# K's weights loaded once and copied to the other half of the partitions by SyncE

## The chip, the core and the metric

The kernel runs on one core of a Trainium2 chip. The core has a matrix engine (TensorE, PE in the profile, its weight loads PEld), three engines for the rest (VectorE: DVE, ScalarE: ACT, GpSimd: POOL), an engine that only issues and synchronizes (SyncE: SP), and 16 DMA engines that serve the transfers which any of them issues. The metric is the device time of one execution in microseconds (us), the median of several runs.

## What is computed

Input x is 8 sequences of 4160 tokens with 192 values in f32. First a causal convolution of 7 taps, with softmaxed weights of each of 8 heads; then a channel mix on its result y:

```python
x_prev = x shifted by one token
xk = mu_k * x + (1.0 - mu_k) * x_prev
xr = mu_r * x + (1.0 - mu_r) * x_prev
k = np.maximum(xk @ w_k, 0.0)          # 192 -> 1024
v = k * k @ w_v                        # 1024 -> 192
r = 1.0 / (1.0 + np.exp(-(xr @ w_r)))  # 192 -> 192
return r * v
```

Here x stands for the convolution's result. The weight of this case is `w_k`, 192 x 1024 in f32, called `wk` in the kernel.

## The kernel before

**Two sequences side by side.** The sequences are taken in four pairs. Of a pair, one sequence lies in partitions 0 to 63 and the other in 64 to 127; the 192 channels are three chunks of 64. A matmul of K uses 64 rows of the array, so two of them, one for each sequence, lie beside each other. That is why `wk` (L179, 128 partitions x 3 chunks x 1024 columns, bf16) holds the same numbers twice, in the lower and in the upper half.

**Steps, slots and bundles.** A pair is cut into steps of 512 tokens; the first step of the first pair has 256. K of a step is made in slots: a slot fills one PSUM buffer with 1024 columns. For the first step a slot covers a quarter of `wk` (256 columns) for 256 tokens, so that slots 0 to 3 need quarters 0 to 3 in turn; later slots cover 128 columns for 512 tokens. For each slot `k_mm` (L465) runs its matmuls, for each chunk first on the lower and then on the upper half; `k_relu` (L489) moves the result out through ScalarE, and `k_square` (L495) squares it on VectorE. Four slots are a bundle. Four PSUM buffers go round among K, the convolution, r and v.

**The order is written out by hand.** Each engine runs its instructions in the order of the program text. `prologue` (L694) issues the first loads, prepares the masks and warms TensorE; `bundle_first` (L738) runs the convolution of the first two groups of x and slots 0 to 3; `bundle_second` (L766) runs slots 4 to 7 and the convolution of group 2; `bundle_rest` goes on from there.

**Who loads what at the start.** The first rows of x come as f32 by ScalarE's and SyncE's queues (`load_x_first`), with the tap weights and `mu`. SyncE then has nothing to issue until the first output. GpSimd issues all loads that change f32 into bf16 under way, in this order: x of group 1 (L712), the quarters of `wk` (L716), x of groups 2 and 3, `wr`, `wv`, x of group 4. `load_wk` (L196) is called once for each quarter and issues two loads of it, one to each half of the partitions; each reads the same part of `w_k` in HBM:

```python
        for c0 in range(0, DF, DF // 4):
            load_wk(c0, c0 + DF // 4)
```

The program's text names no semaphore: the framework makes an instruction wait for the transfers and instructions that wrote what it reads.

Of the kernel before, what the change touches and what calls it, by code (L numbers as in the profile page):

```python
# [14 lines left out]
def kernel(  # L15
# [11 lines left out]
    nc = tc.nc  # L27
# [4 lines left out]
    DF = moe_w_k.shape[1]  # L32
    P = 128
    NF = DF // P
    Q = 64
    NC = D // Q
# [142 lines left out]
    wk = const.tile([P, NC, DF], BF16)  # L179
# [14 lines left out]
            )  # L194

    def load_wk(c0, c1):  # L196
        for st in range(2):
            nc.gpsimd.dma_start(
                out=wk[st * Q : (st + 1) * Q, :, c0:c1],
                in_=bass.AP(  # L200
                    tensor=moe_w_k.tensor,
                    offset=moe_w_k.offset + c0,
                    ap=[[DF, Q], [Q * DF, NC], [1, c1 - c0]],
                ),
            )

    def load_wr():
        load_thirds(wr, moe_w_r, D)
# [485 lines left out]
    def prologue():  # L694
# [21 lines left out]
        for c0 in range(0, DF, DF // 4):  # L716
            load_wk(c0, c0 + DF // 4)
# [183 lines left out]
```

## Time and profile before

| | before |
|---|---|
| time, median of 3 runs | 417.33 us (417.06 to 418.06) |
| span in the profile | 417.0 us |
| GpSimd's DMA queue (q0) | 38704 packets, 14.66 MB |
| SyncE's DMA queue (q1) | 95138 packets, 48.32 MB |
| HBM read and written | 29.89 MB, 36.99 MB |
| loads of `wk` | 8 of 96 KB as written, median 4.7 us from issue to landing |
| mean relu of a slot (L493) | 1038 ns |

The page gives for each engine its busy time, then the span in 40 slices with a digit for the busy tenths of each. Lines of the timeline read: start, duration, engine, source line, operation, output from inputs, shapes, number of instructions, and in brackets the idle time before, with what released the engine. "DMA to landing" is the time from the start of the issuing instruction until the data have arrived. A share of the DMA engines can exceed 100%, since packets overlap within an engine. The chain of waits that the page gives is the work that ended last, followed back from the end.

### The profile page before, as it was taken

Reading aid. Unit: us, or ns where it says so; the run is one execution under the profiler, and the core shown is the slowest. Engines: PE = TensorE matmul, PEld = TensorE weight load, DVE = VectorE, ACT = ScalarE, POOL = GpSimd, SP = SyncE. Lnnn points to the kernel's source line nnn. Section 1 sums busy time; section 2 is a strip of 40 time slices with the busy share of each in tenths; the row PEclk is TensorE's granted clock in tenths of the full one; section 3 lists DMA queues with packets and bytes.
Section 4 is the critical chain, followed back from the end, with each engine's and each line's share of the span. In section 5 each row is a group of like instructions: output and inputs, shape, how many; then the busy total and the mean of one; then the engine's idle time right before and its main releaser. Section 6 shows DMA issues by size and latency. Waiting matters only on the chain.

```text
span 417.0 us, 16363 instructions
## 1 busy us (share of the span) xinstructions
PE 406.8 (98%) x7135; PEld 316.5 (76%) x7136; DVE 377.9 (91%) x672; ACT 347.8 (83%) x408; POOL 52.0 (12%) x79
## 2 busy tenths in 40 slices
PE   7889999999999999999999999999999999999996
PEld 5557777777887777778778877877777787777886
DVE  5888789999999999999999999999999999999984
ACT  6789898898898889889888888988898788877781
POOL 8750003102030100202002010201100000000000
PEclk9999999999999999999999999999999999999999
DMA  9999879958599694959879694797955564411223
GB/s 148 164 191 185 155 215 195 230 139 162 140 185 237 160 190 123 133 169 185 186 139 195 182 174 125 147 234 136 186 105 149 139 160 124 118 62 56 77 79 115
DMA packets 134715, 64.59 MB, mean 155 GB/s; under 512 B 84191, under 2 KB 134643, under 8 KB 134643
## 3 DMA queue, kind: packets, MB, share of 16 engines
q1 hardware_dynamic: 95138, 48.32, 45.4%
q0 software_dynamic: 38704, 14.66, 31.1%
q8 instruction: 56, 0.92, 0.9%
q10 hardware_dynamic: 800, 0.57, 0.5%
q14 instruction: 17, 0.13, 0.1%
HBM read 29.89 MB, written 36.99 MB: 160 GB/s over the span
## 4 chain that ended last, share of the span: by engine, by line
PE 91%; ACT 2%; issue 1%; DVE 0%; ACTq 0%
PE ps_v L566 40%; PE ps_k L481 38%; PE ps_r L538 7%; PE ps_c L299 5%; ACT k_sb L493 1%; PE ps_v L521 1%; ACT y L345 0%; DVE o_sb L582 0%; PE ps_t L390 0%; DVE o_sb L602 0%; ACTq L307 0%; ACTq L345 0%; ACTq L574 0%
## 5 line engine op out<-in xcount | busy, mean ns | idle before, releaser
L493 ACT ACTIVATE k_sb<-ps_k 128x1024 bf16<-128x1024 f32 x260 | 261.2, 1038 | 55.0 <-PE ps_k L481 54.9
L481 PE MATMUL ps_k<-xk,wk 64*128 64x512 bf16 (+1 forms) x1632 | 200.7, 367 | 1.9 <-DMA wk<-in_moe_w_k_dram 1.9
L507 DVE TENSOR_TENSOR k<-k_sb 128x1024 bf16<-128x1024 bf16 x260 | 177.7, 688 | 16.0 <-ACT k_sb L493 8.9
L566 PE MATMUL ps_v<-wv,k 64*128 64x192 bf16 x4032 | 188.8, 243 | 0.6 <-ACT k_sb L493 0.2
L566 PEld LDWEIGHTS <-k 64*128 64x128 bf16 x4032 | 172.4, 94 | 13.6 <-issue 1.2
L481 PEld LDWEIGHTS <-wk 64*128 64x128 bf16 x1632 | 87.9, 94 | 52.2 <-DMA wk<-in_moe_w_k_dram 2.6
L582 DVE TENSOR_TENSOR o_sb<-ps_v,r_sb 128x768 f32<-128x768 f32 x64 | 61.2, 957 | 11.1 <-PE ps_v L566 4.5
L126 POOL DMA_DIRECT2D xb<-in_x_dram x34 | 30.7, 907 | 192.4 <-PE ps_c L299 92.3
L546 ACT ACTIVATE r_sb<-ps_r 128x768 bf16<-128x768 f32 x65 | 54.6, 843 | 0.0
L345 ACT CAST y<-ps_c 120x960 bf16<-120x960 f32 (+4 forms) x67 | 50.7, 787 | 1.7 <-PE ps_c L299 1.7
L538 PEld LDWEIGHTS <-xr 64*128 64x128 bf16 x780 | 36.1, 94 | 12.3 <-issue 1.6
L538 PE MATMUL ps_r<-wr,xr 64*128 64x192 bf16 x780 | 44.0, 243 | 1.2 <-issue 1.1
L299 PE MATMUL ps_c<-xb,toe 64*128 64x480 bf16 (+2 forms) x240 | 39.2, 335 | 0.4
L455 DVE TENSOR_SCALAR xr<-d,mu 128x512 bf16<-128x512 bf16 (+1 forms) x102 | 35.6, 354 | 0.0
L455 DVE TENSOR_SCALAR xk<-d,mu 128x512 bf16<-128x512 bf16 (+1 forms) x99 | 33.2, 362 | 0.1
L424 DVE TENSOR_TENSOR d<-yT 128x1536 bf16<-128x1536 bf16 (+3 forms) x37 | 31.4, 849 | 1.4 <-ACT yT L329 1.4
L461 DVE TENSOR_TENSOR xr<-xr,yT 128x1536 bf16<-128x1536 bf16 (+1 forms) x33 | 31.0, 939 | 1.1
L461 DVE TENSOR_TENSOR xk<-xk,yT 128x1536 bf16<-128x1536 bf16 (+2 forms) x34 | 30.5, 898 | 0.1
L299 PEld LDWEIGHTS <-toe 64*128 64x128 bf16 x240 | 13.5, 94 | 12.4 <-issue 1.3
L408 POOL COPY y_tail<-yT 128x195 bf16<-128x195 bf16 x4 | 1.7, 430 | 68.7 <-DMA yT<-y_dram 68.7
L319 PEld LDWEIGHTS <-xb 128*32 128x32 bf16 (+3 forms) x264 | 4.9, 114 | 2.5 <-ACT xb L220 1.3
L108 POOL MEMSET xb<- 32x384 bf16 x3 | 1.3, 418 | 43.8 <-PE ps_k L481 43.8
(55 smaller groups left out, 62.8 us busy)
## 6 DMA issues: line engine op xcount, KB each, us to landing
out_dram<-o_sb SPq DMA_DIRECT2D x128, 192.0 KB, 2.7
y_dram<-y SPq DMA_DIRECT2D x10, 900.0 KB, 7.6
xb<-in_x_dram POOLq DMA_DIRECT2D x14, 480.0 KB, 8.3
xb<-in_x_dram POOLq DMA_DIRECT2D x6, 432.0 KB, 8.0
xb<-in_x_dram POOLq DMA_DIRECT2D x10, 192.0 KB, 5.6
y_dram<-y SPq DMA_DIRECT2D x3, 450.0 KB
y_dram<-y SPq DMA_DIRECT2D x1, 810.0 KB
wk<-in_moe_w_k_dram POOLq DMA_DIRECT2D x8, 96.0 KB, 4.7
```

What stands on the lines that cost most here:

```text
L299: nc.tensor.matmul(out=banks[:, bank, :, :, k * G : (k + 1) * G], lhsT=toe[q, h, :], rhs=xbs[g][q, :nb, :, h * G : (h + 1) * G], start=hal ...
L345: copy(out=bass.AP(tensor=y.tensor, offset=y.offset + d0, ap=[y.ap[0], [d1 - d0, 2], [2 * D, nb], [Q, 2], [1, n]],), in_=bass.AP(tensor=ps ...
L424: nc.vector.tensor_tensor(out=shaped(s, diffs[s][:, cs, :L]), in0=y_of(s, cs, 1), in1=y_of(s, cs, 0), op=ALU.subtract)
L455: nc.vector.tensor_scalar(out=t[:, c, :L], in0=diffs[s][:, c, :L], scalar1=mu[:, i, c : c + 1], scalar2=None, op0=ALU.mult)
L461: nc.vector.tensor_tensor(out=o, in0=o, in1=y_of(s, sl, 0), op=ALU.add)
L481: nc.tensor.matmul(out=ps[:, i, f * L : (f + 1) * L], lhsT=wk[r, c, fs], rhs=xk[r, c, :L], start=c == 0 and f == 0, stop=c == NC - 1 and f ...
L493: nc.scalar.activation(out=k_sb, in_=ps.rearrange("p a b -> p (a b)"), func=AF.Relu)
L507: nc.vector.tensor_tensor(out=o, in0=i, in1=i, op=ALU.mult)
L538: nc.tensor.matmul(out=ps[:, i, k * D : (k + 1) * D], lhsT=xr[q, c, ts], rhs=wr[q, c, :], start=c == 0, stop=c == NC - 1,)
L546: nc.scalar.activation(out=r_sbs[s, j], in_=ps[:, :, 0 : 2 * D], func=AF.Sigmoid)
L566: nc.tensor.matmul(out=v_ps[s, j][:, bank, k * D : (k + 1) * D], lhsT=k2s[s][q, f, t * P : (t + 1) * P], rhs=wv[q, f, :], start=half == 0 ...
L582: nc.vector.tensor_tensor(out=o_sb.rearrange("p (b t) d -> p b (t d)", b=2), in0=v_ps.pop((s, j)), in1=r_sbs.pop((s, j)), op=ALU.mult,)
```

## The change

`load_wk` loads each quarter only once, into partitions 0 to 63. A second transfer, issued by SyncE, copies the quarter from there to partitions 64 to 127, within on-chip memory and in bf16. It is for reading `w_k` from HBM and converting it once in place of twice, and for taking four transfers from GpSimd's queue. The copy of a quarter reads what the load wrote, so SyncE waits for that load before it issues it. The calls of `load_wk` and all else stay as they are.

```diff
     def load_wk(c0, c1):
-        for st in range(2):
-            nc.gpsimd.dma_start(
-                out=wk[st * Q : (st + 1) * Q, :, c0:c1],
-                in_=bass.AP(
-                    tensor=moe_w_k.tensor,
-                    offset=moe_w_k.offset + c0,
-                    ap=[[DF, Q], [Q * DF, NC], [1, c1 - c0]],
-                ),
-            )
+        nc.gpsimd.dma_start(
+            out=wk[0:Q, :, c0:c1],
+            in_=bass.AP(
+                tensor=moe_w_k.tensor,
+                offset=moe_w_k.offset + c0,
+                ap=[[DF, Q], [Q * DF, NC], [1, c1 - c0]],
+            ),
+        )
+        nc.sync.dma_start(out=wk[Q:P, :, c0:c1], in_=wk[0:Q, :, c0:c1])
```

## The prediction

> **What bounds the kernel now.** I read the page's busy table and slices first, then what touches K's weights (`wk`), then the timeline of TensorE and ScalarE at the start, and last what SyncE's plain transfers take when GpSimd's queue is full.
>
> The page (busy us with share of the span; then busy tenths in 40 slices of 10.4 us):
>
> ```profile
> PE 406.8 (98%) x7135; PEld 316.5 (76%) x7136; DVE 377.9 (91%) x672; ACT 347.8 (83%) x408; POOL 52.0 (12%) x79
> ...
> PE   7889999999999999999999999999999999999996
> ...
> DMA  9999879958599694959879694797955564411223
> ```
>
> TensorE is at 9 everywhere but in the first three slices and the last. The chain of waits is 91% TensorE. So a microsecond lost or won before about 25 us goes to the end nearly one for one, and elsewhere the change touches nothing. In the first four slices the DMA engines are full too.
>
> The view of the tile `wk`, first 60 us (who waited for it: us in total, times):
>
> ```profile
> L198 POOL DMA_DIRECT2D wk<-in_moe_w_k_dram x8: 628/628/687, 4.1 to 8.6; - x8
> ...
>   PEld L481: 2.6, 3
>   PE ps_k L481: 1.9, 2
>   POOL wv L211: 1.0, 1
> ...
> DMA to landing us min/median/max: 4.4/4.7/6.8
> ```
>
> GpSimd issues eight loads, 0.63 us each. TensorE loses 1.9 us in two waits. Where they lie, by TensorE's timeline (start us, us, instruction, [idle before, released by]):
>
> ```profile
> 10.49 1.59 PE L481 MATMUL ps_k<-xk,wk 64*128 64x256 bf16 x25
> 12.44 0.83 PE L481 MATMUL ps_k<-xk,wk 64*128 64x256 bf16 x11 [0.36 <-DMA wk<-in_moe_w_k_dram]
> 14.75 2.40 PE L481 MATMUL ps_k<-xk,wk 64*128 64x256 bf16 x24 [1.49 <-DMA wk<-in_moe_w_k_dram]
> 17.09 1.02 PE L319 MATMUL ps_t<-toe,xb 128*32 128x120 bf16 x64
> ```
>
> and ScalarE's beside it:
>
> ```profile
> 11.36 2.96 ACT L493 ACTIVATE k_sb<-ps_k 128x1024 bf16<-128x1024 f32 x3 [0.20 <-PE ps_k L481]
> 15.90 2.85 ACT L493 ACTIVATE k_sb<-ps_k 128x1024 bf16<-128x1024 f32 x3 [1.58 <-PE ps_k L481]
> ```
>
> The first four slots of K are of step 0 (256 tokens) and need one quarter of `wk` each. Taken one by one, the eight loads, issued at 4.14, 4.82, 5.44, 6.06, 6.68, 7.30, 7.92 and 8.56, took 4.6, 4.7, 4.5, 4.4, 4.4, 5.1, 6.8 and 6.4 us: they landed at 8.7, 9.5, 9.9, 10.5, 11.1, 12.4, 14.7 and 15.0. Slot 3 waits for the last two. The fourth relu starts at 15.90, and from there ScalarE is busy 4.85 of 5 us between 20 and 25 us: nothing downstream makes up lost time. **That start, 15.90, is the number to move.**
>
> **What a plain transfer takes here.** SyncE issues nothing between 2.8 and 30.2 us, so the trace has no such copy at the start. The nearest rows are output stores of 192 KB. Undisturbed, those at 58.86 and 59.30 landed in 2.0 and 2.7 us. Beside GpSimd's loads of x, the first, at 30.23, did this:
>
> ```profile
> L590 SPq DMA_DIRECT2D out_dram<-o_sb x1: 410/410/410, 30.2 to 30.2; - x1
> ...
> DMA to landing us min/median/max: 6.1/6.1/6.1
> ```
>
> The one at 30.68 took 7.3 us. Of two at 77.5 and 78.0 the trace tells one landing, 5.0; of two at 174.6 and 175.1 one, 5.2; two at 150.1 and 150.5 took 5.8 and 6.3. The DMA queues from 31.0 to 33.9 us show why (packets, MB, share of 16 engines; q0 is GpSimd's, q1 SyncE's):
>
> ```profile
> DMA packets 1466, 0.56 MB, mean 192 GB/s; under 512 B 1465, under 2 KB 1465, under 8 KB 1465
> ...
> q0 software_dynamic: 1465, 0.55, 159.5%
> ```
>
> Two stores had been issued, and not one packet of q1 moved in these 2.9 us. From 34.0 to 37.5 us q1 then moved 544 packets (0.39 MB) beside 750 of q0. So a transfer from SyncE first stands some 3 us behind what the engines have already taken from q0, and then shares about one for one.
>
> **What the Trainium skill says.** "DMA: Bandwidth & Descriptors", section "Queues, rings and completion order": each DMA engine goes round the queues that have work and leaves one only at a packet's end. The trace agrees with the sharing from 34 us on, and shows in addition the 3 us before it. The same page, "Two DMAs through the same engine are not ordered": a DMA that reads what another wrote must be issued after the completion semaphore of the first. So the copy adds its whole latency behind the load; no run here shows this pair yet. Same page, "SWDGE vs HWDGE vs iDMA": a cast during the transfer is GpSimd's alone; the loads here do go from f32 to bf16 on GpSimd, and the copy, bf16 to bf16, can go to SyncE. Same page, "Rules for kernel authors": transfers to the two partition halves use the same 16 engines, one transfer of 128 partitions is better. That fits the eight landings above, half a microsecond apart, but the change still makes two transfers of each quarter.
>
> **The change, part by part.**
>
> 1. *Four loads leave GpSimd.* 4 x 0.63 = 2.5 us of issuing. The loads of x for group 2 are issued at 6.7 in place of 9.2, and the wait of 1.0 us before `wv` goes, since fewer GpSimd transfers are in flight. Worth nothing by itself: x of group 2 landed at 16.0 and 17.0 (9.18 and 9.97 + 6.8 to 7.0) and its matmuls came at 17.09 behind K's; if K is late, x is early.
> 2. *The DMA engines' work.* Four loads less, at 0.58 us (8.74 to 10.46 is three of them) 2.3 us of q0. Four copies more: 64 partitions x 3 rows = 192 packets of 512 B each, 768 in all. Undisturbed, q1 moved 287 packets of 768 B in 0.7 us (60.2 to 60.9), so 1.9 us at most. An estimate from these rows: even to 1 us better. It hides behind the same x loads.
> 3. *The first halves.* They keep the places of the first four loads, so the quarters are in the lower partitions at 8.7, 9.5, 9.9 and 10.5. The lower half of quarter 3 comes 4.2 us earlier than now.
> 4. *The copies.* SyncE has finished its own issues at 2.8 and next issues at 30.2, so nothing is queued behind its four waits. Copy 0 goes out at about 8.8. Price: from 2.0 (undisturbed) to 7.3 (the worst above). At 8.8 GpSimd's queue holds three quarters and x of group 2, so I take the disturbed kind, and its lowest, 5.0, since a copy has half the bytes: **copy 0 lands at 13.8**. Copies 1 to 3 are issued by 11 and stand behind it. By bytes (0.39 MB in 3.5 us is 111 KB/us) 96 KB take 0.86 us, by packets (155 a us) 192 take 1.24; I take 1.05. **Copy 3 lands at 13.8 + 3 x 1.05 = 16.95**, against 15.0 for the last load now.
> 5. *The path.* Every slot needs the upper half with its second matmul. Slot 0 starts at 13.8 in place of 10.49. Now the fourth relu starts 0.94 us after the last load (15.90 - 14.96); so 16.95 + 0.94 = 17.9. The other way: slot 0 takes 0.85 us until its relu (10.49 to 11.36), then three relus of 1.03: 13.8 + 0.85 + 3.1 = 17.75. Both say the relu starts at 17.9 in place of 15.90: **+2.0 us**. VectorE's mixing of step 1 ends at 13.7 and isn't what is waited for.
>
> Sum: -0 (issuing) -0 (x earlier, hidden) +2.0 = 417.33 + 2.0 = **419.3 us**.
>
> **The rivals.**
>
> *The copies are hardly disturbed.* For: in a transfer between two parts of on-chip memory no HBM takes part, and a copy has half the bytes of the stores I price from. Against: 2.9 us without one packet can't be due to size. With 2.2 us, copy 0 lands at 11.0 and copy 3 at about 13.0. Then the relus set the pace: 11.0 + 0.85 + 3.1 = 14.95, or 1.0 us before now: 416.3, still within 0.3%. If the earlier x, `wr` and instruction fetches also remove TensorE's stop of 1.14 us at 22.97 (released by "issue", while 16 KB of instructions came through the crowded engines), it is 415.2. This is the case of a win.
>
> *About even.* A copy waits 1.5 us less than I take: 3.5 us, landings at 12.3 and 15.4. Then relu at 16.3, +0.4: 417.7.
>
> *Each copy stands in line on its own.* If every one of the four waits anew behind q0, say 2 us apart, copy 3 lands at 19.8, +4.8: 422. For: 7.3 us for the second of two stores. Against: those two ran without a pause once the first had started.
>
> **How the numbers follow.** Forecast (+1.3 to +3 us) 0.50; even (-1.2 to +1.2) 0.27, in which the undisturbed copy without the removed stop lies; a win of over 0.3% (1.25 us) 0.16; each on its own 0.07. The range from 416.2 to 421.4 leaves out most of the win's 0.16, where it goes below 416.2, and the worst, some 0.2 together. Faster 0.16, same 0.27, slower 0.57.
>
> **What would show it.** Four SyncE issues of `wk<-wk` at about 8.8 to 10.6, with 4.5 to 6.5 us to landing. TensorE's wait for `wk` at L481 up from 1.9 to about 5 us, the first at slot 0 (about 3.3 us), and its releaser the copy, not the load. GpSimd's loads of x of group 2 at 6.7. HBM read down from 29.89 by 0.79 MB, q1 up by some 770 packets. The fourth relu at about 17.9, and the distance to the end from there as now. I am wrong if the copies land within 3 us, if slot 0 starts before 12, or if the relu's delay is made up before 60 us.

## The result and the profile after

The changed kernel takes 421.64 us (median of 4 runs, 421.11 to 423.88), the kernel before 417.19 us beside it. The ratio is 1.0113, with a 95% interval from 1.0074 to 1.0152: **slower by 4.45 us, where 2.0 were forecast.**

The page of the changed kernel (busy us, share, instructions; busy tenths in 40 slices, with the granted TensorE clock in PEclk; then DMA queues with packets, MB, share):

```profile
PE 408.6 (97%) x7135; PEld 317.9 (76%) x7136; DVE 378.1 (90%) x672; ACT 347.6 (83%) x408; POOL 49.4 (12%) x75
...
PE   7699999999999999999999999999999999999996
...
PEclk9899999999999999999999999999999999999999
...
q1 hardware_dynamic: 95970, 48.72, 45.3%
q0 software_dynamic: 37872, 14.26, 30.2%
```

and the same line of the page of before:

```profile
PEclk9999999999999999999999999999999999999999
```

For TensorE the second slice (10.5 to 21.0 us) alone is worse than before. It also shows something that the page of before has nowhere: a granted TensorE clock below 9 tenths. HBM read is 29.10 MB, 0.79 less, as the halved loads must give.

The tile `wk` in the first 60 us, and TensorE's and ScalarE's timelines:

```profile
L205 SPq DMA_DIRECT2D wk<-wk x4: 590/608/735, 8.3 to 11.1; - x4
...
  PEld L481: 3.8, 2
  PE ps_k L481: 3.0, 1
```

```profile
10.79 0.28 PE L481 MATMUL ps_k<-xk,wk 64*128 64x256 bf16 x1
14.09 5.91 PE L481 MATMUL ps_k<-xk,wk 64*128 64x256 bf16 x59 [3.02 <-DMA wk<-wk]
19.93 1.02 PE L319 MATMUL ps_t<-toe,xb 128*32 128x120 bf16 x64
```

```profile
15.58 1.02 ACT L493 ACTIVATE k_sb<-ps_k 128x1024 bf16<-128x1024 f32 x1 [4.11 <-PE ps_k L481]
17.17 5.71 ACT L493 ACTIVATE k_sb<-ps_k 128x1024 bf16<-128x1024 f32 x6 [0.57 <-PE ps_k L481]
```

One matmul of slot 0, on the lower half, runs at 10.79; the next needs the copy and waits 3.02 us. Copies 0, 1 and 3 took 5.7, 6.4 and 6.5 us and landed at 14.04, 15.63 and 17.60 (the trace does not tell copy 2). The first relu above is slot 0's, at 15.58. Relus on end start 0.92 us apart, so the fourth starts at 17.17 + 2 x 0.92 = 19.01. What lay ahead of the copies is told by the DMA queues from 8.9 to 10.8 us, the first fence, and from 11 to 17 us, the second:

```profile
DMA packets 627, 0.24 MB, mean 127 GB/s; under 512 B 560, under 2 KB 627, under 8 KB 627
...
q0 software_dynamic: 627, 0.24, 116.2%
```

```profile
q0 software_dynamic: 2063, 0.77, 109.3%
q1 hardware_dynamic: 825, 0.39, 30.5%
```

Copy 0 was issued at 8.35, and until 10.8 no packet of SyncE's queue moved. Then nearly all of the four copies' packets (825 of 832, 0.39 MB) took six microseconds beside 0.77 MB of GpSimd's.

### The profile page after: what moved, and what is told of

It reads as the page before. It is cut to its first block, busy times and chain, and to the rows that moved or that the text cites. A ratio compares the mean times of both kernels' runs of the same rounds, so it can differ in the third digit from the quotient of the medians.

```text
span 419.2 us, 16367 instructions
## 1 busy us (share of the span) xinstructions
PE 408.6 (97%) x7135; PEld 317.9 (76%) x7136; DVE 378.1 (90%) x672; ACT 347.6 (83%) x408; POOL 49.4 (12%) x75
## 3 DMA queue, kind: packets, MB, share of 16 engines
HBM read 29.10 MB, written 36.99 MB: 158 GB/s over the span
## 4 chain that ended last, share of the span: by engine, by line
PE 90%; ACT 2%; issue 1%; DVE 0%; ACTq 0%
PE ps_v L566 40%; PE ps_k L481 38%; PE ps_r L538 7%; PE ps_c L299 5%; ACT k_sb L493 1%; PE ps_v L521 1%; ACT y L345 1%; DVE o_sb L582 0%; ACT r_sb L546 0%; DVE o_sb L602 0%; ACTq L307 0%; ACTq L345 0%; ACTq L574 0%; ACTq L493 0%
## 5 line engine op out<-in xcount | busy, mean ns | idle before, releaser
L481 PEld LDWEIGHTS <-wk 64*128 64x128 bf16 x1632 | 88.8, 95 | 54.3 <-DMA wk<-wk 3.8
L582 DVE TENSOR_TENSOR o_sb<-ps_v,r_sb 128x768 f32<-128x768 f32 x64 | 61.2, 956 | 11.2 <-PE ps_v L566 4.7
L319 PE MATMUL ps_t<-toe,xb 128*32 128x120 bf16 (+3 forms) x264 | 6.4, 272 | 0.4 <-ACT xb L220 0.4
```

The costliest lines, as they stand in the source:

```text
L481: nc.tensor.matmul(out=ps[:, i, f * L : (f + 1) * L], lhsT=wk[r, c, fs], rhs=xk[r, c, :L], start=c == 0 and f == 0, stop=c == NC - 1 and f ...
L582: nc.vector.tensor_tensor(out=o_sb.rearrange("p (b t) d -> p b (t d)", b=2), in0=v_ps.pop((s, j)), in1=r_sbs.pop((s, j)), op=ALU.mult,)
```

## The experiments

All times are against the kernel before in the same session (417.2 to 417.5 us). In the table "last quarter" is when the last part of `wk` was in place, and "to the end" is the span less the start of the fourth relu, all from the one profiled execution of each.

| run | last quarter | fourth relu | to the end | median us | ratio (95%) |
|---|---|---|---|---|---|
| e0 before again | 14.75 | 15.66 | 400.1 | 417.35 | 1.0001 (0.9991 to 1.0011) |
| the change | 17.60 | 19.01 | 400.2 | 421.64 | 1.0113 (1.0074 to 1.0152) |
| e1 after_warm | 18.32 | 19.43 | 400.2 | 421.54 | 1.0093 (1.0070 to 1.0116) |
| e2 after_drain | 13.76 | 17.14 | 402.7 | 421.88 | 1.0102 (1.0081 to 1.0123) |
| e3 after_gpcopy | 13.79 | 16.05 | 400.9 | 418.47 | 1.0018 (1.0008 to 1.0028) |
| e4 hold_short | 17.93 | 19.48 | 400.5 | 421.01 | 1.0084 (1.0052 to 1.0117) |
| e5 hold_short_warm | 16.46 | 17.37 | 400.3 | 419.64 | 1.0063 (1.0038 to 1.0088) |
| e6 half_dose | 19.55 | 21.09 | 400.6 | 423.90 | 1.0165 (1.0146 to 1.0185) |
| e7 two_copies | 19.63 | 23.37 | 400.3 | 425.27 | 1.0191 (1.0172 to 1.0210) |
| e8 unread | 15.43 | 16.34 | 402.1 | 419.00 | 1.0037 (1.0023 to 1.0051) |
| e9 no_copy | 10.12 | 13.86 | 400.2 | 415.97 | 0.9964 (0.9954 to 0.9973) |
| e10 pool_copy | 12.92 | 14.73 | 401.9 | 418.18 | 1.0014 (1.0002 to 1.0026) |
| e11 dve_copy | 14.78 | 15.70 | 400.6 | 418.09 | 1.0006 (0.9994 to 1.0019) |
| e12 two_dve | 11.63 | 13.74 | 401.2 | 416.82 | 0.9988 (0.9982 to 0.9995) |
| e13 reversed | 13.50 | 18.89 | 400.2 | 420.22 | 1.0064 (1.0048 to 1.0081) |
| e14 reversed_warm | 13.20 | 17.91 | 399.9 | 419.66 | 1.0056 (1.0040 to 1.0072) |

The parts of `wk` in the column "last quarter" are loads or copies, whichever came last. Where nothing later comes late, the column "to the end" is 400.2 within 0.4: a late fourth relu goes to the end one for one.

### A second profile of the kernel before (e0)

No edit.

> The kernel before, unchanged, for a second profile. In the first one TensorE stops for 1.14 us at 22.97 with no releaser but issue; the changed kernel has no such stop. If that stop belongs to the one execution that was profiled, it is absent here, the span is about 1 us shorter (416), and the profiles of before and after are then 3.3 us apart where the first two were 2.2, nearer to the 4.4 us of the times. If the stop belongs to the kernel before, it is here again at the same place, and the changed kernel gains about 1.1 us there. Time 417.2 either way.

The span is 415.8 against 417.0, and the stop at 22.97 shrinks to 0.28 us:

```profile
14.51 2.41 PE L481 MATMUL ps_k<-xk,wk 64*128 64x256 bf16 x24 [1.63 <-ACT k_sb L493]
...
23.01 0.50 PE L538 MATMUL ps_r<-wr,xr 64*128 64x192 bf16 x8 [0.28 <-issue]
```

```profile
15.66 2.86 ACT L493 ACTIVATE k_sb<-ps_k 128x1024 bf16<-128x1024 f32 x3 [1.20 <-PE ps_k L481]
```

So the long stop belonged to one execution. The fourth relu is at 15.66, which makes the change +3.35 there; the spans differ by 419.2 - 415.8 = 3.4, and so do the times of the two profiled runs (421.11 and 417.71).

### Only what stands ahead of the copies is changed (e2, e3, e4)

In e2 GpSimd reads the copied quarters before it goes on to x of group 2; in e4 it reads only the last loaded quarter; in e3 it issues the copies itself, ahead of x of group 2, and SyncE issues none.

```diff
 # e2
         make_toe()
+        hold = const.tile([P, DF // 4], BF16)
+        for c0 in range(0, DF, DF // 4):
+            nc.gpsimd.tensor_copy(out=hold[Q:P, 0:1], in_=wk[Q:P, 0, c0 : c0 + 1])
         load_x(2)
 # e4
+        hold = const.tile([P, 2], BF16)
+        nc.gpsimd.tensor_copy(out=hold[0:Q, 0:1], in_=wk[0:Q, 0, DF - 1 : DF])
         load_x(2)
 # e3
-        nc.sync.dma_start(out=wk[Q:P, :, c0:c1], in_=wk[0:Q, :, c0:c1])
...
             load_wk(c0, c0 + DF // 4)
+        for c0 in range(0, DF, DF // 4):
+            nc.gpsimd.dma_start(out=wk[Q:P, :, c0 : c0 + DF // 4], in_=wk[0:Q, :, c0 : c0 + DF // 4])
```

> The changed kernel, but GpSimd reads one column of each copied quarter (four copies of 64x1 into a spare tile) before it issues x of group 2, so that nothing but K's weights is in GpSimd's DMA queue while SyncE copies. Theory A (the copies stand behind x of groups 2 and 3 in the engines): copy 0 lands within 2.0 to 3.5 us of its issue in place of 5.7, copy 3 at about 13 to 14 in place of 17.6, TensorE's wait at slot 0 falls from 3.0 to under 1.5 us; then x of group 2, issued at about 13.5, comes at about 17 to 18 and sets the start of the convolution of group 2. Fourth relu at about 16, time 417 to 419. Theory B (a copy within on-chip memory takes 5 to 6 us whatever lies beside it): landings as in the changed kernel, copy 3 at 17, x of group 2 only then, time 424 or more.

> The four loads as in the changed kernel; the four copies are issued by GpSimd after them, ahead of x of group 2, in place of SyncE. Theory A (what costs is a second queue that gets its turn only after what the engines have taken from GpSimd's): in one queue the copies stand only behind the loads of K's weights, land 2.5 to 4 us after their issue, copy 0 at about 11.5, copy 3 at about 13.5 to 14.5; x of group 2 is issued at about 11.5 to 12 and lands at 16 to 18. Time 417 to 419. Theory B (the copy itself is dear): 5 to 6 us each, copy 3 at 17 or later, time 421 to 424.

> The changed kernel, but GpSimd reads one column of the last loaded quarter (lower half) before it issues x of group 2, so x of group 2 is issued at about 10.1 in place of 6.7 and most copies are in SyncE's queue first. Loads, copies and their issuer are as in the changed kernel. Theory A (the copies wait for what the engines have taken from GpSimd's queue, whoever issues them): copies land at about 12.4, 12.7, 13.5 and 14 to 15, fourth relu at 16.5 to 17.2 in place of 19.0, x of group 2 at about 16.5 to 17.5; time 418 to 419. Theory B (a transfer from SyncE behind one from GpSimd is dear in itself): copy 0 again after 5 us or more, time 421 or more.

The transfers `wk<-wk` of e2, first their times to landing, then the DMA queues from 9.95 to 13.5 us:

```profile
DMA to landing us min/median/max: 2.1/3.1/3.7
```

```profile
q1 hardware_dynamic: 832, 0.39, 44.3%
```

With only the loads of K's weights ahead of them, the same four transfers from SyncE land in 2.1 to 3.7 us, the last at 13.76. e3 has the same range from the other queue: 2.1 to 3.7 us, the last at 13.79. e4 shows both kinds within one run. Copies 0 and 1, issued at 9.5 and 10.3, ahead of x of group 2 (11.2), took 3.0 and 3.1 us; copy 3, issued at 12.5, behind it, took 5.4. So neither SyncE nor the on-chip copy is dear by itself: **what the copies wait for is the loads of x that were issued before them.**

The times were less well foreseen. e2's copies are early, but its slots run at a granted clock of 0.50 from 14 to 16 us, so that the fourth relu comes only 1.9 us earlier; and x of group 2, issued at 14.3, lands at 18.0 and 19.6, and TensorE stops 1.3 us for it. So it is 402.7 to the end, and the whole gain is gone. In e4 the last copy still stands behind x. e3 wins back 3.2 of the 4.2 us; what is left shows in the fourth relu, 0.4 us later than in e0, and in `wv`, which lands at 24.3 and keeps TensorE waiting for 0.8 us.

### Half the dose, and fewer, longer packets (e6, e7)

e6 loads quarters 0 and 1 twice, as before, and copies quarters 2 and 3 alone. e7 copies quarter 0, and then quarters 1 to 3 in one transfer.

```diff
 # e6
+        if c0 < DF // 2:
+            nc.gpsimd.dma_start(out=wk[Q:P, :, c0:c1], in_=...)
+        else:
             nc.sync.dma_start(out=wk[Q:P, :, c0:c1], in_=wk[0:Q, :, c0:c1])
 # e7
+        if c0 == 0:
             nc.sync.dma_start(out=wk[Q:P, :, c0:c1], in_=wk[0:Q, :, c0:c1])
+        elif c1 == DF:
+            nc.sync.dma_start(out=wk[Q:P, :, DF // 4 : DF], in_=wk[0:Q, :, DF // 4 : DF])
```

> Quarters 0 and 1 loaded twice by GpSimd as before, quarters 2 and 3 loaded once and copied by SyncE. Slots 0 and 1 start at about 10.7 as before, so TensorE does not idle ahead of slot 0. Theory A (the landing of the last copy sets the fourth relu): copies issued at about 11.3 and 12, 5 to 6 us each, copy 3 at 17 to 18, fourth relu at about 18 to 19, time 419.5 to 421. Theory B (what costs is the late slot 0 with four relus after it and the clock that is halved there): fourth relu at most 1 us later than before, time 418 to 418.5.

> The changed kernel with quarter 0 copied alone and quarters 1 to 3 in one copy of 64 partitions x 3 runs of 1536 bytes: half the packets, the same bytes. Theory A (SyncE's packets take turns with GpSimd's one for one, so it is the number of packets that counts): copy 0 at about 14, the second, issued at about 11, with 192 packets at about 15.5 to 16.3, against 17.6 for the last of four; then relus at ScalarE's pace from slot 0, or at the half clock's, fourth relu at 17.8 to 18.8, time 420 to 421. Theory B (bytes count, or the wait ahead of each transfer): the second lands at 17.5 or later, time 421.6 or more.

Half the copies cost more than all of them, and more than either expectation allowed. In e6 they are issued at 11.4 and 12.3, when x of groups 2 and 3 is in the queue whole (landing, then TensorE):

```profile
DMA to landing us min/median/max: 6.5/6.9/7.3
```

```profile
17.98 1.46 PE L491 MATMUL ps_k<-xk,wk 64*128 64x256 bf16 x12 [5.42 <-DMA wk<-wk]
```

Slots 0 and 1 were on time there, so a late slot 0 is not what costs: the last copy is. e7 lends no support to the idea of turns by packets: a third of the packets for the same bytes, and 8.3 us for the second transfer, about what copies 1 to 3 of the change took from the first issue to the last landing (9.2 to 17.6). It was issued 2 us later than copy 1 of the change, with more loads issued ahead of it, so whether bytes or packets count is not settled.

### The two halves of the change by themselves (e8, e9)

e8 is the kernel before with the four copies into a tile that nobody reads. e9 is the change without copies: K of the odd sequences takes its weights from the tile of the convolution's taps (`toe`), and so their output is not computed.

```diff
 # e8, on the kernel before
+        nc.sync.dma_start(out=wk2[Q:P, :, c0:c1], in_=wk[0:Q, :, c0:c1])
 # e9, on the change
-        nc.sync.dma_start(out=wk[Q:P, :, c0:c1], in_=wk[0:Q, :, c0:c1])
...
-                        lhsT=wk[r, c, fs],
+                        lhsT=wk[r, c, fs] if i == 0 else toe[r, (j * nf + f) % H, :],
```

> The kernel before, with its eight loads, and in addition SyncE's four copies of the lower half, into a tile that nothing reads. So the copies and their traffic are there, and no matmul waits for them. Theory A (the loss is the wait for the copies, not their traffic): copies land 5 to 8 us after their issue, TensorE does not wait for them, and the time is 417.2 to 417.9 (0.77 MB more traffic for a moment, up to 0.5 us on loads 7 and 8). Theory B (the copies slow the loads of x and of the instructions, and that is the loss): time 419 or more.

> The changed kernel without its copies: the four loads are halved as in the change, and K's second matmul of each pair (odd sequences) takes its weights from the tile of the convolution's taps in place of the upper half of wk; so the odd sequences of the output are not computed. It shows what the change would bring if the upper half came at no cost. Theory A (the removed loads had a price of their own, which the copies' wait outweighs): slot 3 is ready with the fourth load at 10 to 11, the fourth relu starts at 14.5 to 14.9 (ScalarE's pace), x of group 2 lands by 14, time 416 to 416.6. Theory B (the removal of the loads is worth nothing, since x of group 2 or ScalarE binds next): 416.9 to 417.5.

e9 takes 415.97 us: the four removed loads are worth 1.5 us (ratio 0.9964) where no copy has to be waited for. e8 takes 419.00: the copies' presence costs 1.5 us even where nobody waits for them. In its profile the last load of `wk` lands at 15.4 in place of 14.75, and that is 0.7 us of the path. The second half of x of group 2 lands at 18.4 in place of 16.7, but TensorE has no idle time for it. What more is lost there is TensorE's pace, which the next part is about: after a wait of 2.43 us the granted clock is 0.50 from 17 to 20 us, and 64 matmuls of the convolution take nearly twice as long, first in e0, then in e8:

```profile
16.85 1.02 PE L319 MATMUL ps_t<-toe,xb 128*32 128x120 bf16 x64
```

```profile
18.30 1.92 PE L321 MATMUL ps_t<-toe,xb 128*32 128x120 bf16 x64
```

The profiled execution (420.37) is one of five of e8's fifteen with a mean clock of 0.996 or less; the other ten have a median of 418.7, so without that loss the cost is some 1.2 us. The forecast had both parts at zero. They are not, and in these two kernels they are of equal size; e8's copies ran beside eight loads, though, so that they cancel in the change itself is not shown.

### TensorE's pace (e1, e5, e13, e14)

Each "warm" kernel runs matmuls of zeros ahead of slot 0, into the buffer that slot 0 starts anew: 14 in e1, 8 in e5 (which is otherwise e4), 18 in e14. e13 and e14 have no copies; they are the kernel before with the quarters loaded in reverse order, so that slot 0 waits for the last load.

```diff
 # e1, e5, e14 (n is the slot)
+        if n == 0:
+            for i in range(14):
+                nc.tensor.matmul(out=ps[:, i % 2, :], lhsT=ones_t, rhs=zeros, start=True, stop=True)
 # e13, e14
-        for c0 in range(0, DF, DF // 4):
+        for c0 in reversed(range(0, DF, DF // 4)):
```

> The changed kernel, with 14 matmuls of zeros ahead of slot 0 of K, so that TensorE works while it waits for the first copy. They write a PSUM buffer that slot 0 then starts anew, so the result is as before. Theory A (TensorE's idle 3.0 us halve its granted clock, which makes slots 0 to 2 take 1.3 us each in place of 0.65): the granted clock stays at 1.00 from 14 to 18 us, slot 1 is ready 0.6 us and the fourth relu about 0.8 us earlier (18.4 in place of 19.2), time 421.6 - 0.8 = 420.8. Theory B (only the copies' landings set the path, the clock is not on it): the clock may stay up, but the time stays at 421.6.

> As e4_hold_short, with 8 matmuls of zeros ahead of slot 0, so that TensorE has no idle stretch while it waits for copy 0. Theory C (the halved clock after an idle stretch is on the path when the copies land early, since slots then take 1.28 us each, more than ScalarE's 0.92): granted clock 1.00 throughout, fourth relu 0.7 to 1.1 us before that of e4_hold_short, time lower by as much. Theory D (the clock is not on the path): same time as e4_hold_short within 0.4 us.

> The kernel before with its eight loads in the reverse order of the quarters (3, 2, 1, 0). No copy and no other traffic; slot 0 now waits for the last load, at about 14.8, and TensorE idles some 4 us ahead of it. Theory C (idle before K halves TensorE's pace and that is on the path when all quarters are there): slots of 1.3 us each for some 3.4 us, fourth relu at about 19 to 19.5, 421 to 421.7. Theory D (pace is not on the path): relus at ScalarE's 0.92, fourth at 18.4, 420.2.

> As e13_reversed, with 18 matmuls of zeros ahead of slot 0 that fill TensorE's idle stretch. The loads are the same. Theory C: slots of 0.65 us, fourth relu at about 18.4, 0.7 to 1.1 us before that of e13_reversed, and the time lower by as much. Theory D: no difference of more than 0.4 us.

The matmuls of K in the changed kernel, in stretches of 2 us (us, TensorE busy and count, weight loads, granted clock, DMA share, GB/s):

```profile
14.00:16.00 2.00, 1.78 (x16) 0.98 (x18) 0.53 1.46 203
16.00:18.00 2.00, 2.00 (x26) 1.45 (x24) 0.61 1.52 197
```

After 3.0 us of idling the granted clock is about half, until 17.5. TensorE's timeline in e13, and then in e14:

```profile
13.27 6.98 PE L481 MATMUL ps_k<-xk,wk 64*128 64x256 bf16 x60 [2.02 <-DMA wk<-in_moe_w_k_dram]
```

```profile
10.29 4.06 PE L477 MATMUL ps_k<-zeros,ones_t 128*128 128x512 bf16 x18
14.28 4.09 PE L484 MATMUL ps_k<-xk,wk 64*128 64x256 bf16 x60
```

The same 60 matmuls take 6.98 us after an idle stretch of 2.0, and 4.09 without one. The zeros ran 1.1 us longer than the loads took to land (13.20), and still the fourth relu is 1.0 us earlier, 17.91 against 18.89. In the times that is 419.66 against 420.22, with overlapping ranges (419.29 to 420.90, 419.37 to 421.08): clear in the profiles, only suggested by the times. e5 is also below e4 (419.64, 421.01), but its last copy landed 1.5 us earlier as well, so most of that is not pace. "TensorE: Matmul & The Clock Gate" of the Trainium skill, section "What's actually happening", has the array at half rate once it has idled for a window of about 3.4 us. The half is seen here, but the length of the idling alone does not decide. In e13 2.0 us were enough; in e4 0.6 us, and K's first matmul there had taken 0.39 in place of 0.28 us already before that idling; in e0 slot 3 ran at full pace after 1.63 us. Slots 0 and 1 in e4, and then in e5:

```profile
12.53 2.74 PE L481 MATMUL ps_k<-xk,wk 64*128 64x256 bf16 x24 [0.60 <-DMA wk<-wk]
```

```profile
12.78 1.59 PE L484 MATMUL ps_k<-xk,wk 64*128 64x256 bf16 x25
```

The small matmuls of the convolution that ran before may be part of it (not tried).

On the path of the change it is worth little. From the last copy to the fourth relu it is 1.41 us in the changed kernel, 1.55 in e4 and 1.54 in e6, against 0.91 in e0 and e5, which ran at full pace: **0.5 us** by the profiles. The times do not show it: e1, where slots 0 and 1 ran at full pace, won nothing, and its last copy landed at 18.32 in place of 17.60.

### Copies without a transfer (e10, e11, e12)

e10 copies on GpSimd after x of group 2 is issued; e11 on VectorE, two quarters before the mixing of step 1 and two within it. e12 copies quarters 0 and 1 alone on VectorE and loads quarters 2 and 3 twice. SyncE copies nothing in the three.

```diff
 # e10
         load_x(2)
+        for c0 in range(0, DF, DF // 4):
+            nc.gpsimd.tensor_copy(out=wk[Q:P, :, c0 : c0 + DF // 4], in_=wk[0:Q, :, c0 : c0 + DF // 4])
 # e12, in bundle_first, ahead of slot 0 (e11 does the same by a helper)
+        for c0 in (0, DF // 4):
+            c1 = c0 + DF // 4
+            nc.vector.tensor_copy(out=wk[Q:P, :, c0:c1], in_=wk[0:Q, :, c0:c1])
 # e12, on the kernel before
-        for st in range(2):
+        for st in range(2 if c0 >= DF // 2 else 1):
```

> The four loads of the change; the upper half is copied by GpSimd itself (a tensor copy of 64 x 768 for each quarter, from partitions 0 to 63 to 64 to 127), after it has issued x of group 2. No second transfer, no place in any DMA queue. Theory A (a transfer's latency behind GpSimd's queue is the whole loss, so a copy without a transfer wins what the removed loads are worth): if such a copy takes 1.0 to 1.3 us, the quarters are there at about 9.7, 10.9, 12.1 and 13.3, the fourth relu starts at 14.3 to 14.8, x of group 3 is issued at 13.5 and still comes in time: 416 to 417. Theory B (the copies on GpSimd take 2 us or more each, or hold up its issuing of x of group 3, wr and wv): the fourth relu at 16 or later or a stop for wv, 417.5 to 420.

> The four loads of the change; the upper half is copied by VectorE, 64 x 768 for each quarter, quarters 0 and 1 after the mixing of step 0, quarters 2 and 3 between the parts of the mixing of step 1. No second transfer and nothing more on GpSimd. Theory A (the wait for a transfer is the loss; the removed loads are worth 1.5 us, as e9_no_copy showed): if a copy takes 0.3 to 0.5 us, the four relus of bundle 0 run on end from about 11.5, the mixing of step 1 ends at 14.7 to 15.5, and slot 4's relu, the first that feels it, starts at 15.5 to 16.3 against 16.6 in the kernel before; time 416.3 to 417.2, ahead of both kernels. Theory B (VectorE is full there and a copy takes 0.8 us or more): the mixing ends after 16.5, time 417.5 to 419.

> Quarters 0 and 1 loaded once and copied to the upper half by VectorE after the mixing of step 0; quarters 2 and 3 loaded twice by GpSimd as before: six loads, no transfer between halves. Theory A (two loads less take away most of what the last two loads cost, and VectorE has 0.5 us to spare ahead of step 1): copies of 0.5 us end at about 10.7, the sixth load lands at about 11.6 to 12.4, the four relus run on end, the fourth starts at about 14.3 to 14.6, the mixing of step 1 ends at 14.4 and slot 4's relu starts at 15.2 to 15.6 against 16.6 in the kernel before: 416.2 to 416.9, ahead of both kernels. Theory B (VectorE's 0.6 us comes back elsewhere, or the sixth load comes late on one engine): 417 to 418.

e10's quarters are there by 12.9 and its four relus run on end, but the next thing is late. VectorE's mixing of step 1 in e0, and then in e10 beside GpSimd's copies (9.5 to 12.9):

```profile
10.18 0.43 DVE L424 TENSOR_TENSOR d<-yT 128x512 bf16<-128x512 bf16 x1 [0.50 <-ACT yT L329]
10.64 0.43 DVE L455 TENSOR_SCALAR xk<-d,mu 128x512 bf16<-128x512 bf16 x1
11.11 0.45 DVE L461 TENSOR_TENSOR xk<-xk,yT 128x512 bf16<-128x512 bf16 x1
```

```profile
10.54 0.87 DVE L423 TENSOR_TENSOR d<-yT 128x512 bf16<-128x512 bf16 x1 [0.87 <-ACT yT L328]
11.44 0.80 DVE L454 TENSOR_SCALAR xk<-d,mu 128x512 bf16<-128x512 bf16 x1
12.28 0.92 DVE L460 TENSOR_TENSOR xk<-xk,yT 128x512 bf16<-128x512 bf16 x1
```

The same instructions take twice as long, and slot 4 waits for the mixing until 15.9. In e11 the last copy, queued behind VectorE's own work, ends at 14.8: no gain. e12 has two loads less and VectorE's half microsecond of idle time for the copies:

```profile
10.98 3.77 ACT L493 ACTIVATE k_sb<-ps_k 128x1024 bf16<-128x1024 f32 x4 [0.53 <-PE ps_k L481]
15.25 1.94 ACT L493 ACTIVATE k_sb<-ps_k 128x1024 bf16<-128x1024 f32 x2 [0.50 <-DVE k L507]
```

Four relus on end from 10.98, and 416.82 us against 417.50: **e12 is ahead of both kernels**; against the kernel before it is a ratio of 0.9988 (0.9982 to 0.9995), some 0.5 us.

## Why the forecast was right and where it failed

The direction, the mechanism and the place held: the copies wait behind x, and the path is the last copy's landing, the fourth relu, the end. Of the signs named for being wrong none came, but for the one matmul of slot 0 at 10.79. The size did not hold: +2.0 us were forecast and +4.45 measured. Two steps failed: step 4 priced the copies too low (copy 3 at 16.95, measured 17.60), and step 5 put TensorE's loss of pace after the wait at nothing (0.94 us from the last copy to the relu, measured 1.41).

- *Step 1, GpSimd's issuing*: x of group 2 was issued at 6.66, as forecast. "Worth nothing by itself" failed: e9 shows 1.5 us for the removed loads, where the last quarter is there at 10.1 and not at 14.75.
- *Step 2, the engines' work, "hides behind the same x loads"*: failed by as much the other way, 1.5 us in e8. That the two are of equal size in these kernels, so that the sum's zero was not far off, was luck.
- *Step 3, the first halves*: forecast at 8.7, 9.5, 9.9 and 10.5; measured at 8.3, 8.8, 9.4 and 11.1.
- *Step 4, the copies' price*: **this is the largest term that was mis-sized, by 0.65 us.** I took 5.0 us for copy 0, the lowest of the disturbed stores, because it has half the bytes; it took 5.7 (from an earlier issue: 14.04 against 13.8). I took 1.05 us from copy to copy; it was (17.60 - 14.04) / 3 = 1.19. Copy 3 landed at 17.60, and at 18.32 in e1. Half the bytes brought no discount: the 5.7 to 6.5 us of the copies lie among the 5.0 to 7.3 of the disturbed stores, and e2 and e6 (2.1 against 7.3 us for the same bytes) show that what stands in the queue at the time sets the price.
- *Step 5, the path*: the 0.94 us were taken over unchanged; at half pace it is 1.41, another 0.47 us. Nothing in the forecast asked what 3 us of idling do to TensorE.
- *The baseline*: the first profile's last load (14.96) and fourth relu (15.90) were a little late, the relu by 0.24 us against e0. With 0.65 and 0.47 this leads from 2.0 to 3.35. Against e0 the sum closes: landing 17.60 - 14.75 = 2.85, pace 0.50, together 3.35, and the spans differ by 3.4.

From 3.4 to the 4.45 of the medians about 1.0 is left, and it lies in which executions were profiled: that of the changed kernel (421.11) is 0.5 us below its median, that of e0 (417.71) 0.5 us above the 417.19. What the unprofiled executions lose is not seen. Later copies are likely, since e1, whose profiled time (421.53) lies at the median, has its last copy 0.7 us later. More time at half pace is the other candidate: half the clock for 3.4 us of 419 makes an estimated mean of 0.996, which three executions have, and the slowest, 423.88, has 0.991. How the 1.0 us divide stays open.

Of the rivals, undisturbed copies need a queue without x (e2), which the change does not have there; "each copy stands in line on its own" gave 422, near the time, but its copy 3 at 19.8 was not seen. Of the signs named ahead, the issues at 8.3 to 11.1, their 5.7 to 6.5 us, 3.0 us at slot 0, x of group 2 at 6.7, HBM's 0.79 MB and q1's 832 more packets came true. TensorE's waits for `wk` did not reach 5 us: only the 3.0 are counted as waits, since at half pace slots 0 and 1 themselves fill the time until the next copies.

## What to carry to other kernels

A transfer that depends on another one is issued late by its nature, and pays for whatever loads have been queued by then: look up what else is in the DMA engines at that moment, and price it by the deepest queue that it can meet, not by its bytes alone. Ask of each part of a change what it does alone: here two parts of 1.5 us each had been put at nothing, and a version that keeps some of one without the other (e12, two loads less and no transfer) is the one that wins. When a wait ahead of matmuls grows, count the pace after it too.

## What the runs showed of the hardware

- Transfers of 96 KB from SyncE, all the same: 2.1 us with the engines empty (e2), 5.7 to 6.5 in the change, 7.3 behind two groups of x (e6).
- TensorE's pace fell to about half after idling of 3.0 us in the change and 2.0 in e13, and it can stay low while the matmuls go on: 60 matmuls in 6.98 us in e13, against 4.09 without the idling. e4, slow after 0.6 us, and e0, at full pace after 1.6, show that idling is not the whole cause. In e13 the record of the granted clock shows 1.00 all the while, where the changed kernel's shows 0.53; the matmuls' own times are the surer sign.
- GpSimd's copies between on-chip tiles doubled the duration of VectorE's instructions beside them (0.43 to 0.87 us). "SBUF — State Buffer" of the Trainium skill, section "Who interferes with whom", says that the two engines exclude each other where VectorE reads two on-chip operands or runs in a mode that takes both ports; the doubling agrees.
- Two executions of the kernel before differ in TensorE's stop at 23 us: 1.14 us in one, 0.28 in the other (e0).
